# Mamba-2 scan with a cosine router: the start of the scan reordered, with work moved from VectorE and ScalarE to GpSimd

## The chip, the cores and the metric

The kernel runs on one core of one Trainium2 chip. The metric is the device time of one execution in microseconds (us), median of several runs. Before the change it is 239.88 us over three runs (239.1, 239.88 and 241.01).

The engines are TensorE (in the profile PE, and PEld for its weight loads), VectorE (DVE), ScalarE (ACT), GpSimd (POOL) and SyncE (SP), which here issues nearly all loads. Each engine works through its own queue in order. A wait in front of an instruction holds everything behind it on that engine.

## The reference, cut to what matters

Two blocks are chained: a state-space scan and a layer of eight experts.

```python
# scan; batch 4, heads 8, seq 768, head_dim 32, d_state 16
cum = np.cumsum(np.log(np.clip(a, 1e-06, 1.0)), axis=-1)      # within a chunk
M = np.einsum('bhin,bhjn->bhij', Cc, Bc) * np.exp(cum_i - cum_j) * causal
y = M @ xc + np.exp(cum_i) * (Cc @ state)
state = decay_full * state + sum_j(decay_from_j * Bc_j * xc_j)
# router and experts; 3072 tokens of 256, 8 experts with F = 1024
logits = normalize(x) @ normalize(expert_emb).T / tau
out[mask_e] = gate * (np.maximum(x[mask_e] @ w1[e], 0) @ w2[e])
```

The result does not depend on the length of the chunk, and the kernel uses chunks of 128 tokens (`Q`), so there are six of them (`NC`), for all four batches (`NB`) and eight heads at once.

## The kernel before, in words

**Two parts.** The scan, `mamba` (line 776), runs first and writes one row per token to DRAM. The experts, `moe`, follow: rows are gathered per expert and multiplied with its weights. The change touches the scan alone, and in it `begin_scan` (line 723), which prepares chunk 0, and the constants that are built there.

**How a chunk is computed.** The factor exp(cum_i - cum_j) is split in two. `decays` (line 242) turns the input `a` into products of decays `f`, taken from the middle of the chunk (`HQ` = 64), and `inverse` (line 267) takes 1/f as `r`, on VectorE. TensorE spreads `f` to the layout of C with a matrix of zeros and ones (`spread_decays`, line 283): four batches by four chunks are 16 matmuls, chunks 0 and 1 to the two banks of `py`, chunks 2 and 3 to the two of `pz`. `scale_c` (line 315) multiplies C by that on VectorE and gives `cp`. `turn_inverse` (line 273) transposes `r` on TensorE, and ScalarE copies it to `rT`. `scale_x` (line 324) multiplies x by it and gives `xs`.

Then come pairs of batches. Pair p is chunk p // 2, batches 0 and 1 or 2 and 3. For each pair:

- `scores` (line 607): 16 matmuls of B by `cp`, into the PSUM tiles `pgA` and `pgB`. B stands in `bz` in two copies, each with the rows of the other half zeroed. For chunks 0 and 1 `split_b` (line 226) makes the copies on ScalarE from a plain load `in_b`, by a multiplication with the masks `tmask`. From chunk 2 on, DMAs of single rows write straight into `bz`, which `clear_b` (line 156) zeroed on ScalarE.
- `masks` (line 620): the causal mask. VectorE multiplies `pgA` by the mask. ScalarE copies `pgB` to the SBUF tile `g`, and GpSimd zeroes the upper triangle there (`affine_select`, line 631).
- `outputs` (line 636): 16 matmuls (32 records, each fp32 matmul is two passes) of `xs` by `g` into `py`. From the third record pair on they need GpSimd's half of `g`.
- `sums` (line 670), once per chunk: B by `xs`, which gives the new state, and `tokens` (line 701), which turns the outputs to rows.

The next pair's `scores` write `pgA` and `pgB` again, so they wait until `masks` of this pair has read them.

**What sets the order.** The order on each engine is the order in which the code calls these functions (a hand-made schedule); waits are put in by the framework. `begin_scan` (lines 744 to 773) issues, in this order: the constants of the later routing (`place_consts`, all on GpSimd), the decays, `split_b(0)`, the spread, `inverse`, `scale_c(0)` for two batches and two more, `scale_x(0)`, `scores(0)`, some fill matmuls on zeros (line 239), the squares of the router's embeddings (line 363, ScalarE, and a power on GpSimd, line 364), `masks(0)`, `split_b(1)`, `scale_c(1)`, `scores(1)`, `masks(1)`.

**Loads.** SP issues them in the order of the calls, and a load may also wait for the load eight places earlier, because eight semaphores are used in turn. `in_b`, `in_c` and `in_x` are B, C and x of a chunk in the layouts of the scan; `in_t` is B by token.

## Time and profile before

| | |
|---|---|
| median of three runs | 239.88 us (239.1 to 241.01) |
| the profiled execution | 238.6 us, of which the span of the trace is 236.9 us |
| granted TensorE clock, mean | 0.992 of full speed |
| busy, share of the span | PE 95%, DVE 75%, ACT 54%, POOL 41% |
| instructions | 6602 |

The rows of the trace are read so: start in us from the span's start, duration in us, engine, line of the code, operation, output <- input with partitions x elements, and the number of merged instructions. In square brackets stands how long the engine had been idle and what ended that. "Mean ns" in a grouped row is the mean duration of one instruction. A row for a DMA shows the issue; its landing is in a view of its own.

### The profile page before, as it was taken

Reading aid. Unit: us, or ns where it says so; the run is one execution under the profiler, and the core shown is the slowest. Engines: PE = TensorE matmul, PEld = TensorE weight load, DVE = VectorE, ACT = ScalarE, POOL = GpSimd, SP = SyncE. Lnnn points to the kernel's source line nnn. Section 1 sums busy time; section 2 is a strip of 40 time slices with the busy share of each in tenths; the row PEclk is TensorE's granted clock in tenths of the full one; section 3 lists DMA queues with packets and bytes.
Section 4 is the critical chain, followed back from the end, with each engine's and each line's share of the span. In section 5 each row is a group of like instructions: output and inputs, shape, how many; then the busy total and the mean of one; then the engine's idle time right before and its main releaser. Section 6 shows DMA issues by size and latency. Waiting matters only on the chain. (4 is left out here: it accounts for less than half of the span.)

```text
span 236.9 us, 6602 instructions
## 1 busy us (share of the span) xinstructions
PE 224.1 (95%) x2500; PEld 211.2 (89%) x2500; DVE 178.5 (75%) x468; ACT 129.0 (54%) x348; POOL 98.0 (41%) x125
## 2 busy tenths in 40 slices
PE   7899989999999799999999999999999999999980
PEld 7788878877899699999999999999999999999970
DVE  6997968997875628697868788877887978874850
ACT  6867665762621445653684468358456456647620
POOL 8736211263027507536427334631841643305113
PEclk9999999999999999999999999999999999999996
DMA  5879675565607832626246233724626444201002
GB/s 176 280 230 299 236 185 163 155 196 164 233 13 261 295 116 69 209 75 187 78 148 190 82 133 114 238 63 166 192 80 203 144 140 148 93 3 61 0 3 64
DMA packets 20978, 34.83 MB, mean 147 GB/s; under 512 B 2474, under 2 KB 13968, under 8 KB 20944
## 3 DMA queue, kind: packets, MB, share of 16 engines
q1 hardware_dynamic: 18256, 27.97, 36.9%
q0 software_dynamic: 2592, 6.39, 8.5%
q8 instruction: 20, 0.33, 0.6%
q14 instruction: 14, 0.11, 0.2%
q10 hardware_dynamic: 96, 0.03, 0.1%
HBM read 28.02 MB, written 6.42 MB: 145 GB/s over the span
## 5 line engine op out<-in xcount | busy, mean ns | idle before, releaser
L1135 POOL DMA_INDIRECT out_dram<-yo,to x26 | 29.4, 1130 | 60.7 <-ACT yo L1134 46.4
L1058 DVE TENSOR_TENSOR hT<-bank,hp 128x416 f32<-128x416 f32 (+6 forms) x42 | 22.1, 553 | 14.8 <-ACT hp L1052 9.7
L908 POOL DMA_INDIRECT xg<-rows,table x24 | 27.9, 1162 | 7.0 <-issue 4.5
L1052 ACT COPY hp<-bank 128x416 f32<-128x416 f32 (+6 forms) x42 | 19.9, 475 | 17.7 <-PE bank L1039 17.3
L1064 ACT ACTIVATE hT<-hT 128x416 f32<-128x416 f32 (+6 forms) x42 | 21.6, 525 | 11.3 <-DVE hT L1058 11.2
L1000 DVE TENSOR_TENSOR ws<-w 128x512 f32<-128x512 f32 x42 | 27.6, 685 | 0.0
L631 POOL TENSOR_SCALAR_AFFINE_SELECT g<-g 128x1024 f32<-128x1024 f32 x13 | 16.3, 1257 | 25.9 <-ACT g L630 25.9
L1039 PE MATMUL bank<-ts,w 128*128 128x208 f32 (+6 forms) x112 | 21.8, 328 | 0.0
L1039 PE MATMUL bank<-xT,w 128*128 128x208 f32 (+6 forms) x112 | 21.6, 326 | 0.0
L1100 PE MATMUL bank<-ts,w 128*128 128x208 f32 (+6 forms) x112 | 21.4, 334 | 0.0
L1039 PE MATMUL bank<-ts,ws 128*128 128x208 f32 (+6 forms) x112 | 20.5, 326 | 0.0
L1100 PE MATMUL bank<-ts,ws 128*128 128x208 f32 (+6 forms) x112 | 19.5, 326 | 0.0
L1100 PE MATMUL bank<-hT,w 128*128 128x208 f32 (+6 forms) x112 | 19.5, 326 | 0.0
L1100 PEld LDWEIGHTS bank<-ts,w 128*128 128x128 f32 x112 | 18.1, 190 | 0.9 <-DVE ts L1004 0.2
L1004 DVE TENSOR_TENSOR ts<-hT 128x416 f32<-128x416 f32 (+6 forms) x28 | 15.0, 556 | 5.1 <-ACT hT L1064 4.1
L1039 PEld LDWEIGHTS bank<-xT,w 128*128 128x128 f32 x112 | 18.8, 190 | 0.0
L1039 PEld LDWEIGHTS bank<-ts,ws 128*128 128x128 f32 x112 | 18.5, 190 | 0.1
L923 POOL TENSOR_TENSOR gr<-gr,half 128x3 f32<-128x3 f32 (+2 forms) x9 | 9.2, 1022 | 22.4 <-ACT sq L919 13.2
L1039 PEld LDWEIGHTS bank<-ts,w 128*128 128x128 f32 x112 | 18.0, 190 | 0.5 <-ACT hp L1052 0.4
L1100 PEld LDWEIGHTS bank<-hT,w 128*128 128x128 f32 x112 | 18.4, 190 | 0.0
L1100 PEld LDWEIGHTS bank<-ts,ws 128*128 128x128 f32 x112 | 18.4, 190 | 0.0
L1004 DVE TENSOR_TENSOR ts<-hT,ts 128x416 f32<-128x416 f32 (+6 forms) x28 | 14.9, 551 | 0.2
(256 smaller groups left out, 496.5 us busy)
## 6 DMA issues: line engine op xcount, KB each, us to landing
w<-in_moe_w_dram SPq DMA_DIRECT2D x28, 512.0 KB, 3.5
rows<-yt SPq DMA_DIRECT2D x12, 264.0 KB, 2.9
in_x<-in_x_dram SPq DMA_DIRECT2D x6, 512.0 KB, 5.0
w<-in_moe_w_dram SPq DMA_DIRECT2D x8, 256.0 KB, 3.6
in_c<-in_CT_dram SPq DMA_DIRECT2D x6, 256.0 KB, 4.2
in_t<-in_B_dram SPq DMA_DIRECT2D x6, 256.0 KB, 3.7
bz<-in_BT_dram SPq DMA_DIRECT2D x16, 64.0 KB, 4.9
in_b<-in_BT_dram SPq DMA_DIRECT2D x2, 256.0 KB, 3.3
```

Source lines behind the costliest of these rows:

```text
L631: nc.gpsimd.affine_select(out=g, in_=g, pattern=[[0, 8], [1, Q]], compare_op=ALU.is_ge, fill=0.0, base=0, channel_multiplier=-1)
L908: s.k.nc.gpsimd.indirect_dma_start(out=s.x[0:p, i, 0:TOK], out_offset=None, in_=rows, in_offset=bass.IndirectOffsetOnAxis(ap=s.at[0:p, i : ...
L923: nc.gpsimd.tensor_tensor(out=s.r[:], in0=s.r[:], in1=k.half[:, 0:nt], op=ALU.pow)
L1000: s.k.nc.vector.tensor_tensor(out=o, in0=in0, in1=in1, op=op)
L1004: s.k.nc.vector.tensor_tensor(out=t[i], in0=in0, in1=in1, op=ALU.subtract)
L1039: k.nc.tensor.matmul(out[:, g], lhsT=lhsT[:, f : f + 128], rhs=rhs, start=(g == 0 and i in (1, 2, 5)), stop=True, skip_group_check=True,)
L1052: nc.scalar.copy(out=u.p[:, {1: 0, 6: 1, 7: 2}[i]], in_=u.a)
L1058: nc.vector.tensor_tensor(out=out, in0=in0, in1=u.p[:, q], op=ALU.add)
L1064: s.k.nc.scalar.activation(c, c, ACT.Relu)
L1100: k.nc.tensor.matmul(out, lhsT=lhsT, rhs=rhs, start=(i in (1, 2) and f == 0), stop=(f == half - 1), skip_group_check=True)
L1135: d = nc.gpsimd.indirect_dma_start(out=k.out[:, :], out_offset=bass.IndirectOffsetOnAxis(ap=s.to[0:p, i : i + 1], axis=0), in_=y[:p], in_o ...
```

## The change

**First decays.** `spread_decays` takes the batches to be spread. Batches 0 and 1 are spread first, for chunks 0 to 3, then 2 and 3. Of chunk 0, batches 0 and 1 go to `pgA[:, 0]`, a bank that nothing else uses then. VectorE scales C for batches 0 and 1 from there, and for 2 and 3 from `py`. Four matmuls of one column (`spread_last`) bring the last decay of chunk 0 to `py`, where the copy to `fr` reads it.

**Inverse in two pieces.** The reciprocal is taken for columns 0 to 63 before the first `scale_c` and for 64 to 127 after the second one. The transposition comes after `scores(0)`, in a place of `pz[0]`.

**Order of VectorE.** `masks(0)` and `scale_c(1)` stand ahead of `scale_x(0)`. VectorE does the half of `xs` for batches 0 and 1, GpSimd the half for 2 and 3. The copy of one column of C for chunk 1 goes from VectorE to ScalarE.

**GpSimd.** It makes the two copies of B of chunk 1 (`split_b` with `scalar=False`), ahead of its first mask. The constants of the routing are no longer built at the start but in four portions after the masks of steps 2 to 5.

**Zeroing of `bz`.** Before: two copies on ScalarE of 1024 elements per partition. Now one of 1536 on ScalarE, at the start, and a memset of 512 on VectorE.

**Loads.** x of chunk 0 comes in two halves, and B of chunk 1 is loaded before C of chunk 1.

The core of the diff:

```diff
-    clear_b(k, 2)
+    k.nc.scalar.copy(
+        out=k.bz[:, 2:4].rearrange("p c v b m -> p (c v b) m")[:, 0 : 3 * NB], in_=bc(k.zero[:, 0:Q], [128, 3 * NB, Q], 1)
+    )
...
+    v.memset(k.bz[:, 3, 1].rearrange("p b m -> p (b m)"), 0.0)
...
+        h = m // 2 if n == "x" and c == 0 else m
+        for o in range(0, m, h):
+            k.nc.sync.dma_start(v[:].rearrange("p b m -> p (b m)")[:, o : o + h], src[:, o : o + h])
...
-def split_b(k, c):
+def split_b(k, c, scalar=True):
...
+        if scalar:
+            k.nc.scalar.activation(t.bz[:, v], t.bt[:], ACT.Copy, scale=k.tmask[:, v : v + 1])
+        else:
+            flat = lambda a: a.rearrange("p b m -> p (b m)")
+            k.nc.gpsimd.tensor_scalar(
+                out=flat(t.bz[:, v]), in0=flat(t.bt[:]), scalar1=k.tmask[:, v : v + 1], scalar2=None, op0=ALU.mult
+            )
...
-def inverse(k, kk):
+def inverse(k, kk, cut=slice(0, Q)):
...
+def spread_last(k):
     for b in range(NB):
+        k.nc.tensor.matmul(
+            k.py[:, 0, b : b + 1], lhsT=k.spread[0:32, b, :], rhs=k.f[0:32, 0, Q - 1 : Q], start=True, stop=True,
+            tile_position=(0, 0),
+        )
...
+            at = k.pgA[:, 0] if c == 0 and b < 2 else spread_at(k, c)
...
-def scale_x(k, c, lo=0, n=NB):
+def scale_x(k, c, lo=0, n=NB, vector=True):
...
-    load(k, 1, "cb")
+    load(k, 1, "bc")
...
-    turn_consts(k)
-    next(consts)
-    next(consts)
     next(first)
     next(first)
+    inverse(k, 0, slice(0, HQ))
     split_b(k, 0)
-    clear_b(k, 3)
     load_two(k, 2)
-    spread_decays(k, range(4))
-    inverse(k, 0)
-    scale_c(k, 0, spread_at(k, 0), 0, 2)
-    turn_inverse(k, 0, k.pgB[:, 1, 384:512])
+    turn_consts(k)
+    split_b(k, 1, scalar=False)
+    spread_decays(k, range(4), (0, 1))
+    scale_c(k, 0, k.pgA[:, 0], 0, 2)
+    spread_decays(k, range(4), (2, 3))
     scale_c(k, 0, spread_at(k, 0), 2, 2)
-    scale_x(k, 0)
-    scores(k, 0)
+    inverse(k, 0, slice(HQ, Q))
     keep_decays(k, 2)
     keep_decays(k, 3)
+    scores(k, 0)
+    spread_last(k)
+    masks(k, 0)
+    turn_inverse(k, 0, k.pz[0][:, 384:512])
     fill(k, 3, k.pz[0][:, 0:Q])
...
-    norm_embeddings(k)
-    masks(k, 0)
-    split_b(k, 1)
     scale_c(k, 1, spread_at(k, 1))
     t = k.ld[1]
-    nc.vector.tensor_copy(out=t.cp[:, :, HQ : HQ + 1], in_=t.ct[:, :, HQ : HQ + 1])
+    nc.scalar.copy(out=t.cp[:, :, HQ : HQ + 1], in_=t.ct[:, :, HQ : HQ + 1])
+    scale_x(k, 0, 0, 2)
+    scale_x(k, 0, 2, 2, vector=False)
+    norm_embeddings(k)
     scores(k, 1)
     masks(k, 1)
-    k.later = later
+    k.later, k.consts = later, consts
...
         if 1 < s and not last:
             masks(k, s, () if s in (3, 9) else (1,))
+        if 1 < s:
+            next(k.consts, None)
```

How the instructions stand on three queues. The names left of the arrow are outputs; the waits are the semaphores that stand in front of an instruction. On VectorE, from the last step of the decays (`f`) to the mask of pair 1, before:

```order
L263 MEMSET f 32x1 [waits DVE_49]
L269 RECIPROCAL r<-f 128x128 [waits DVE_49]
L270 MEMSET r 128x1 [waits DVE_49]
L321 TENSOR_TENSOR cp<-in_c,py 128x256 [waits DMAHW5_49,PE_49]
L321 TENSOR_TENSOR cp<-in_c,py 128x256
L330 TENSOR_TENSOR xs<-in_x,rT 128x1024 [waits DMAHW6_49,Activation_49]
L628 TENSOR_TENSOR g<-pgA,mask 128x1024 [waits PE_49,Pool_49]
L321 TENSOR_TENSOR cp<-in_c,py 128x512 [waits DMAHW3_49,Activation_49]
L770 COPY cp<-in_c 128x4 [waits DVE_49]
L628 TENSOR_TENSOR g<-pgA,mask 128x1024 [waits PE_49]
```

and now:

```order
L277 MEMSET f 32x1 [waits DVE_49]
L283 RECIPROCAL r<-f 128x64
L346 TENSOR_TENSOR cp<-in_c,pgA 128x256 [waits DMAHW5_49,PE_49]
L346 TENSOR_TENSOR cp<-in_c,py 128x256 [waits PE_49]
L283 RECIPROCAL r<-f 128x64 [waits DVE_49]
L285 MEMSET r 128x1 [waits DVE_49]
L653 TENSOR_TENSOR g<-pgA,mask 128x1024 [waits PE_49,Pool_49]
L346 TENSOR_TENSOR cp<-in_c,py 128x512 [waits DMAHW5_49,PE_49,Activation_49]
L355 TENSOR_TENSOR xs<-in_x,rT 128x512 [waits DMAHW6_49]
L653 TENSOR_TENSOR g<-pgA,mask 128x1024 [waits PE_49]
```

`xs` has moved from ahead of the first mask to behind the scaled C of chunk 1, and only half of it is left; the copy of one column is gone.

On GpSimd, around its first mask of the scan (`g`), before:

```order
L125 IOTA step_i 128x32
L127 CAST step<-step_i 128x32 [waits Pool_49]
L151 MEMSET width 128x1 x8
L364 TENSOR_TENSOR emb_r<-emb_r,half 8x1 [waits Activation_49]
L631 AFFINE_SELECT g<-g 128x1024 [waits Activation_49] x2
```

and now:

```order
L381 COPY turn<-ident 128x2x32 x2
L242 TENSOR_SCALAR bz<-in_b_154,tmask 128x512 [waits DMAHW4_49]
L242 TENSOR_SCALAR bz<-in_b_154,tmask 128x512
L656 AFFINE_SELECT g<-g 128x1024 [waits Activation_49]
L355 TENSOR_TENSOR xs<-in_x,rT 128x512 [waits DMAHW7_49,Activation_49]
L389 TENSOR_TENSOR emb_r<-emb_r,half 8x1 [waits Activation_49,Pool_49]
L656 AFFINE_SELECT g<-g 128x1024 [waits Activation_49]
```

The constants are gone from the stretch; the two copies of B, with a wait for a load, stand ahead of the first mask, and half of `xs` ahead of the second.

On SP, the loads behind those of x of chunk 0, before:

```order
L347 DMA tau<-in_moe_tau_dram 8x1 [waits DMAHW2_49]
L177 DMA in_c<-in_CT_dram 128x512 [waits DMAHW3_49]
L177 DMA in_b_160<-in_BT_dram 128x512 [waits DMAHW4_49]
L177 DMA in_t<-in_B_dram 128x512 [waits DMAHW5_49]
L166 DMA a_92<-in_a_dram 32x128 [waits DMAHW6_49]
```

and now:

```order
L372 DMA tau<-in_moe_tau_dram 8x1 [waits DMAHW3_49]
L185 DMA in_b_154<-in_BT_dram 128x512 [waits DMAHW4_49]
L185 DMA in_c<-in_CT_dram 128x512 [waits DMAHW5_49]
L185 DMA in_t<-in_B_dram 128x512 [waits DMAHW6_49]
L172 DMA a_92<-in_a_dram 32x128 [waits DMAHW7_49]
```

The load of C of chunk 1 now waits for semaphore 5, which the load of C of chunk 0 raises; before, B by token (`in_t`) stood at that wait.

More of the change, by code (lines that the diff above doesn't have):

```diff
@@ L106, in early_consts, with late_consts @@
     )
-    before = m.tile([128, 128], F32, name="before")
+    k.half = c.tile([128, NU], F32, name="half")
+    g.memset(k.half[:], 0.5)
+def late_consts(k):
+    c, g = k.const, k.nc.gpsimd
+    before = k.mc.tile([128, 128], F32, name="before")
     g.affine_select(
-        out=before[:], in_=ones[:, 0:128], pattern=[[1, 128]], compare_op=ALU.is_gt, fill=0.0, base=0,
+        out=before[:], in_=k.ones[:, 0:128], pattern=[[1, 128]], compare_op=ALU.is_gt, fill=0.0, base=0,
         channel_multiplier=-1,
     )
-    k.half = c.tile([128, NU], F32, name="half")
-    g.memset(k.half[:], 0.5)
     k.ones_b = c.tile([128, 128], BF16, name="ones_b")
@@ L128, in ramp @@
         return f
+    k.xg = [c.tile([128, NT, 2 * Y1], F32, name=f"xg{i}") for i in range(3)]
+    late_consts(k)
+    yield
     k.lows = ramp("lows", 128, BF16)
@@ L142, in place_consts @@
     nc.gpsimd.memset(k.acc[:], 0.0)
+    yield
     k.shift_f = c.tile([128, E], F32, name="shift_f")
@@ L151, in place_consts @@
         nc.gpsimd.memset(k.width[:, r : r + 1], float(w + PAD if r == 0 else w))
-    k.xg = [c.tile([128, NT, 2 * Y1], F32, name=f"xg{i}") for i in range(3)]
     yield
-def clear_b(k, i):
-    k.nc.scalar.copy(out=k.bz[:, i], in_=bc(bc(k.zero[:, 0:Q], [128, NB, Q], 1), [128, 2, NB, Q], 1))
 def load_decays(k, c, engine):
@@ L229, in split_b @@
     for v in range(2):
-        k.nc.scalar.activation(t.bz[:, v], t.bt[:], ACT.Copy, scale=k.tmask[:, v : v + 1])
+        if scalar:
[5 more added lines that the diff above has]
+            )
 def fill(k, n, at=None):
@@ L264, in decays @@
     yield
-def inverse(k, kk):
+def inverse(k, kk, cut=slice(0, Q)):
     p = slice(0, 64 if kk else 128)
-    k.nc.vector.reciprocal(out=k.r[p, kk], in_=k.f[p, kk])
-    k.nc.vector.memset(k.r[p, kk, HQ : HQ + 1], 1.0)
+    k.nc.vector.reciprocal(out=k.r[p, kk, cut], in_=k.f[p, kk, cut])
+    if cut.stop == Q:
+        k.nc.vector.memset(k.r[p, kk, HQ : HQ + 1], 1.0)
 def turn_inverse(k, kk, ps):
@@ L280, in spread_at, with spread_decays @@
     return (k.py[:, 0], k.py[:, 1], k.pz[0], k.pz[1], k.py[:, 0], k.py[:, 1])[c]
-def spread_decays(k, chunks):
+def spread_last(k):
     for b in range(NB):
+        k.nc.tensor.matmul(
+            k.py[:, 0, b : b + 1], lhsT=k.spread[0:32, b, :], rhs=k.f[0:32, 0, Q - 1 : Q], start=True, stop=True,
+            tile_position=(0, 0),
+        )
+def spread_decays(k, chunks, batches=range(NB)):
+    for b in batches:
         for c in chunks:
             g = 32 * (c % 4)
+            at = k.pgA[:, 0] if c == 0 and b < 2 else spread_at(k, c)
             k.nc.tensor.matmul(
-                spread_at(k, c)[:, 128 * b : 128 * b + 128], lhsT=k.spread[g : g + 32, b, :],
+                at[:, 128 * b : 128 * b + 128], lhsT=k.spread[g : g + 32, b, :],
                 rhs=k.f[g : g + 32, c // 4, :], start=True, stop=True, tile_position=(g, 0),
@@ L329, in scale_x @@
     r = k.rT[:, c // 4, 32 * (c % 4) + 8 * lo : 32 * (c % 4) + 8 * lo + 8 * n]
-    k.nc.vector.tensor_tensor(
+    (k.nc.vector if vector else k.nc.gpsimd).tensor_tensor(
         out=t.xs[:, b].rearrange("p b h d -> p (b h) d"), in0=t.x[:, b].rearrange("p b (h d) -> p (b h) d", h=NH),
@@ L744, in begin_scan @@
     first, later, consts = decays(k, 0), decays(k, 1), place_consts(k)
-    turn_consts(k)
-    next(consts)
-    next(consts)
     next(first)
     next(first)
+    inverse(k, 0, slice(0, HQ))
     split_b(k, 0)
-    clear_b(k, 3)
     load_two(k, 2)
-    spread_decays(k, range(4))
-    inverse(k, 0)
-    scale_c(k, 0, spread_at(k, 0), 0, 2)
-    turn_inverse(k, 0, k.pgB[:, 1, 384:512])
+    turn_consts(k)
[3 more added lines that the diff above has]
+    spread_decays(k, range(4), (2, 3))
     scale_c(k, 0, spread_at(k, 0), 2, 2)
-    scale_x(k, 0)
-    scores(k, 0)
+    inverse(k, 0, slice(HQ, Q))
     keep_decays(k, 2)
     keep_decays(k, 3)
+    scores(k, 0)
+    spread_last(k)
+    masks(k, 0)
+    turn_inverse(k, 0, k.pz[0][:, 384:512])
     fill(k, 3, k.pz[0][:, 0:Q])
-    nc.scalar.copy(out=k.fr[:, 0, :, Q - 1 : Q], in_=by_batch(spread_at(k, 0))[:, :, Q - 1 : Q])
+    nc.scalar.copy(out=k.fr[:, 0, :, Q - 1], in_=k.py[:, 0, 0:NB])
     nc.scalar.copy(out=k.fr[:, 1, :, HQ:Q:63], in_=by_batch(spread_at(k, 1))[:, :, HQ:Q:63])
-    norm_embeddings(k)
-    masks(k, 0)
-    split_b(k, 1)
     scale_c(k, 1, spread_at(k, 1))
     t = k.ld[1]
-    nc.vector.tensor_copy(out=t.cp[:, :, HQ : HQ + 1], in_=t.ct[:, :, HQ : HQ + 1])
+    nc.scalar.copy(out=t.cp[:, :, HQ : HQ + 1], in_=t.ct[:, :, HQ : HQ + 1])
+    scale_x(k, 0, 0, 2)
+    scale_x(k, 0, 2, 2, vector=False)
+    norm_embeddings(k)
     scores(k, 1)
     masks(k, 1)
-    k.later = later
+    k.later, k.consts = later, consts
 def mamba(k):
```

1 line of the change is left out of this document (removed).

## The prediction

> **What bounds the kernel now.** I read the busy time by stretches of the span first (us of the stretch, then busy time and instructions of PE, PEld, DVE, ACT and POOL, granted clock, DMA share, GB/s).
>
> ```profile
> 16.00:68.00 52.00, 49.98 (x1248) 42.91 (x1248) 42.96 (x102) 30.09 (x58) 15.29 (x12) 1.00 0.61 189
> 68.00:231.00 163.00, 160.65 (x996) 156.50 (x995) 122.61 (x332) 87.05 (x269) 69.43 (x61) 1.00 0.40 127
> ```
>
> From 16 us on TensorE is busy 96% and then 99% of the time at full clock. So whatever moves the start of that stretch moves the end by as much, and nothing else in this change can. The price of the change is how much earlier or later TensorE gets into its unbroken run. That is read from the timeline of the first 16 us:
>
> ```profile
> 6.42 0.75 DVE L321 TENSOR_TENSOR cp<-in_c,py 128x256 f32<-128x256 f32 x2
> 6.99 0.38 PE L614 MATMUL pgA<-cp,bz 32*128 32x128 f32 x2 [0.27 <-DVE cp L321]
> 7.37 1.23 DVE L330 TENSOR_TENSOR xs<-in_x,rT 128x1024 f32<-128x1024 f32 x1 [0.20 <-DMA in_x<-in_x_dram]
> 7.96 0.28 PE L614 MATMUL pgB<-cp,bz 32*128 32x128 f32 x2
> 8.17 0.94 PE L239 MATMUL pz<-zero 128*128 128x128 f32 x6
> 8.40 0.98 ACT L630 COPY g<-pgB 128x1024 f32<-128x1024 f32 x1
> 8.52 1.22 DVE L628 TENSOR_TENSOR g<-pgA,mask 128x1024 f32<-128x1024 f32 x1
> 9.25 0.58 POOL L364 TENSOR_TENSOR emb_r<-emb_r,half 8x1 f32<-8x1 f32 x1
> 9.65 0.68 DVE L321 TENSOR_TENSOR cp<-in_c,py 128x512 f32<-128x512 f32 x1
> 9.79 0.38 PE L614 MATMUL pgA<-cp,bz 32*128 32x128 f32 x2 [0.69 <-DVE g L628]
> 9.81 1.09 POOL L631 TENSOR_SCALAR_AFFINE_SELECT g<-g 128x1024 f32<-128x1024 f32 x1
> 10.36 0.56 DVE L770 COPY cp<-in_c 128x4 f32<-128x4 f32 x1
> 10.89 1.13 PE L657 MATMUL py<-g,xs 128*32 128x128 f32 x32
> 11.00 1.23 DVE L628 TENSOR_TENSOR g<-pgA,mask 128x1024 f32<-128x1024 f32 x1
> ```
>
> The chain is: scaled C at 6.42, scores(0) from 6.99 to 8.24 (7.96 + 0.28), VectorE's mask from 8.52, because `xs` holds VectorE until 8.60, to 9.74, scores(1) at 9.79. TensorE's last real wait is the 0.69 us ahead of 9.79; the fill matmuls at 8.17 are also waiting. From 9.79 it runs on: outputs(0) at 10.89, which needs GpSimd's part of the mask, done at 9.81 + 1.09 = 10.90. The same timeline a little later:
>
> ```profile
> 12.14 1.09 POOL L631 TENSOR_SCALAR_AFFINE_SELECT g<-g 128x1024 f32<-128x1024 f32 x1 [1.24 <-ACT g L630]
> 12.39 0.38 PE L614 MATMUL pgA<-cp,bz 32*128 32x128 f32 x2
> 13.50 0.65 PE L657 MATMUL py<-g,xs 128*32 128x128 f32 x16
> 14.05 1.22 DVE L628 TENSOR_TENSOR g<-pgA,mask 128x1024 f32<-128x1024 f32 x1
> 14.79 1.09 POOL L631 TENSOR_SCALAR_AFFINE_SELECT g<-g 128x1024 f32<-128x1024 f32 x1 [1.57 <-ACT g L630]
> 15.18 0.98 DVE L695 TENSOR_TENSOR T<-V,whole 128x256 f32<-128x256 f32 x1
> ```
>
> Scores(2) start at 12.39 and outputs(1) at 13.50, with GpSimd's second mask done at 13.23, in time. I carry the sum to these places.
>
> **The change part by part.** First the loads, since two instructions now wait for them (issue rows, then the median from issue to landing of single loads: C of chunk 0, x of chunk 0, B of chunk 1):
>
> ```profile
> 2.16 0.43 SPq L177 DMA_DIRECT2D in_c<-in_CT_dram  x1
> 2.64 0.43 SPq L177 DMA_DIRECT2D in_x<-in_x_dram  x1
> 4.96 0.43 SPq L177 DMA_DIRECT2D in_b<-in_BT_dram  x1
> in_c<-in_CT_dram SPq DMA_DIRECT2D x1, 256.0 KB, 3.9
> in_x<-in_x_dram SPq DMA_DIRECT2D x1, 512.0 KB, 4.6
> in_b<-in_BT_dram SPq DMA_DIRECT2D x1, 256.0 KB, 4.1
> ```
>
> C of chunk 0 lands at 2.16 + 3.9 = 6.06, x at 7.24, B of chunk 1, queued behind C of chunk 1, at 9.06.
>
> *First decays by batch.* Scaled C for batches 0 and 1 no longer waits for all 16 spread matmuls, but cannot start before C is there: 6.10 instead of 6.42. The gain is 0.32, not the half of the spread. Scores(0) followed 0.57 after it (6.42 to 6.99) and took 1.25, so they run 6.67 to 7.92. Splitting the inverse takes the second half off this path; it lies under scores(0).
>
> *Mask ahead of `xs`.* The mask starts when scores(0) end, at about 8.05 (gain 0.47), and ends at 9.27; scores(1) start at 9.32. The four matmuls of one column and the moved transposition stand in TensorE's wait, ahead of the fill; between 7.92 and 9.32 there are 1.40 us, of which the fill takes 0.94. If they take more than the remaining 0.46, scores(1) slip: 0 at best, 0.2 at worst. I take 0, because the step below comes out later in any case.
>
> *GpSimd.* Its queue is now: two copies of B (128x512), mask, half of `xs`, power, mask. B of chunk 1 has moved one place forward. C and B of chunk 1 are equal in size and landed between 7.24 and 9.06, so I put the first at half way, 8.15, and the bounds at 7.6 and 9.06; C now takes the second place, 9.06, just before it is needed at 9.27. For the copies there is no row. The nearest ones, and the two that show ScalarE's side and VectorE's prices:
>
> ```profile
> 2.99 0.29 POOL L97 TENSOR_SCALAR_AFFINE_SELECT ident<-ident 128x128 f32<-128x128 f32 x1
> 9.29 1.33 ACT L230 ACTIVATE bz<-in_b,tmask 128x512 f32<-128x512 f32 x2
> 17.69 0.69 DVE L321 TENSOR_TENSOR cp<-in_c,fr 128x512 f32<-128x512 f32 x1
> 23.90 0.41 DVE L695 TENSOR_TENSOR T<-V,whole 128x256 f32<-128x256 f32 x1
> 26.90 1.09 POOL L631 TENSOR_SCALAR_AFFINE_SELECT g<-g 128x1024 f32<-128x1024 f32 x1 [3.09 <-ACT g L630]
> 27.03 2.04 DVE L330 TENSOR_TENSOR xs<-in_x,rT 128x1024 f32<-128x1024 f32 x1
> ```
>
> From 0.29 at 128 elements to 1.09 at 1024 a copy of 512 takes 0.65; half of 1.09, 0.54, and 0.75 are the bounds. Two copies: 8.20 to 9.50. ScalarE's part of the mask, which is no longer behind the transposed inverse, ends at 8.05 + 0.98 = 9.03. So GpSimd's mask runs 9.50 to 10.59, against 10.90 before. What was taken from ScalarE (1.33) has become GpSimd's bound.
>
> *VectorE against GpSimd.* The rows show that the two engines exclude each other on some operations. `T` takes 0.41 alone (23.90), but 0.98 when it meets a mask on GpSimd: 14.79 + 1.09 = 15.88, and `T` ends at 16.16, 0.28 later. `xs` takes 1.23 alone and 2.04 at 27.03: it ends 1.08 after GpSimd's mask does. The little copy at 10.36 took 0.56 and ended with GpSimd's mask. The mask on VectorE, which reads PSUM, keeps its 1.22 at 14.05. So an operation of VectorE with both inputs in SBUF stands still until GpSimd's instruction is over, and saves some 0.13 of its start. The Trainium skill, "SBUF — State Buffer", section "Who interferes with whom", states it as a rule: a VectorE instruction with two SBUF inputs and a GpSimd instruction that reads SBUF share a read port, and the one that issues second blocks fully. By that rule the new half of `xs` cannot lie under GpSimd's mask; without it the half would cost its 0.69 and no more. The rows above bear the rule out.
>
> VectorE has scaled C of chunk 1 by 9.18 + 0.69 = 9.87 and would start its half of `xs` at 9.9. GpSimd's mask began at 9.50, so it waits until 10.59 and ends at 10.59 + 0.69 - 0.13 = 11.15. Outputs(0) need it: they start at 11.25 instead of 10.89, a loss of 0.36. The gain of 0.47 is not lost ahead of that point but is spent in this wait. Mask(1) then runs 11.15 to 12.38, ahead of scores(2) at 12.39 + 0.36 = 12.75.
>
> *Half of `xs` on GpSimd.* It comes after VectorE's half. It reads two tensors of 512, as many elements as the mask's 1024, so I take 1.09; bounds 0.65 (one input) and 1.3 (two such). 11.15 to 12.24, before the second half of the sums needs it at about 12.5. The power, 0.58, ends at 12.82 and the second mask at 13.91. Outputs(1) start at 13.50 + 0.36 = 13.86 and need it with their third matmul: another 0.1. With the bounds of the half this is 0 to 0.3. The Trainium skill, "GPSIMD Engine Reference", section 3.1, gives 4497 ns for a two-input operation of 2048 elements, about twice VectorE; a quarter of that is 1.12 by estimate, and the sum would stay. No row of this trace has such an operation on GpSimd.
>
> *Hidden edits.* The constants of the routing were GpSimd's work from 3.77 to 9.30, with no one waiting. Their first and last rows, two gaps ahead of later masks, and two rows for the zeroing of `bz`:
>
> ```profile
> 3.11 1.03 ACT L157 COPY bz<-zero 128x1024 f32<-128x1024 f32 x1
> 3.34 0.23 DVE L250 TENSOR_SCALAR aw<-a 128x126 f32<-128x126 f32 x1 [0.87 <-DMA a<-in_a_dram]
> 3.77 0.40 POOL L108 TENSOR_SCALAR_AFFINE_SELECT before<-ones 128x128 f32<-128x128 f32 x1
> 8.96 0.34 POOL L151 MEMSET width<- 128x1 f32 x8
> 18.50 3.00 POOL L631 TENSOR_SCALAR_AFFINE_SELECT g<-g 128x1024 f32<-128x1024 f32 x2 [2.62 <-ACT g L630]
> 22.73 1.09 POOL L631 TENSOR_SCALAR_AFFINE_SELECT g<-g 128x1024 f32<-128x1024 f32 x1 [1.22 <-ACT g L630]
> ```
>
> At most 5.5 us in four portions, some 1.4 each at the longest, go into gaps of which these two and the 3.09 above are three. If a portion of 1.4 met the gap of 1.22, that mask would be 0.2 late; I take 0. ScalarE's zeroing of 1536 elements takes about half as long again, 3.11 to 4.66, and its two copies of B of chunk 0, 1.33, end at 6.0, ahead of scores(0); if they were later than 6.67, each 0.1 would cost as much. VectorE's memset lies in the 0.87 us of waiting for `a`. The extra load costs SP one issue of 0.43; B of chunk 1 is issued where C stood, plus that, and both wait behind x of chunk 0 anyway.
>
> **The sum.** -0.47 up to the first mask, +0.83 for the wait of `xs` (from -0.47 to +0.36), +0.1 at the second mask of GpSimd: +0.46. The profiled execution took 238.6 us (span 236.9) and would take 239.06. The median of the three runs shown, 239.88, is 1.28 above that execution, so I forecast 239.88 + 0.46, rounded to 240.3 us.
>
> **The rivals.**
>
> *A, the forecast:* GpSimd's queue takes the place of ScalarE's and VectorE's. 240.3 us.
>
> *B, the gain comes through.* If B of chunk 1 lands at the early bound, 7.6, and each copy takes 0.54, GpSimd's mask starts at 9.08 with ScalarE's and ends at 10.17. The half of `xs` ends at 10.73, outputs(0) start at 10.83, near 0. If the half also gets in ahead of that mask, it ends at 10.6 and the gain is up to 0.47, less what the second mask gives back. For it speaks that scores(0) really start earlier; against it the 9.06 of the load. Between 0 and -0.47 I put it at -0.3: 239.6 us.
>
> *C, the port goes the wrong way.* If GpSimd's next instruction, its own half of `xs`, is served at 10.59 ahead of the waiting half of VectorE, this one begins 1.09 later, ends at 12.24, and outputs(0) start at 12.34: +1.45, so 241.3 us. It decides as soon as VectorE's half arrives while the mask of GpSimd is running, as in A. The rows show VectorE waiting behind a single instruction of GpSimd, never behind two in a row, so they cannot exclude it.
>
> *D, the change does nothing:* the moved matmuls and the fill push scores(1) back to 9.8 and what remains cancels. 239.9 us. For it speaks the narrow 0.46; against it that the fill has only to end, not to be followed by a wait.
>
> **How the numbers follow.** A 0.45, B 0.30, C 0.15, D 0.10. All four lie within 0.7% of 239.88. A measurement of this kernel can tell about 1% from no change (2.4 us), and its three runs lie 1.9 us apart. The range takes in B and C and half of that scatter: 238.9 to 241.6. Beyond 1% only something outside these cases would reach: 0.04 for faster, 0.05 for slower (C together with copies at 0.75 and a late load), 0.91 within.
>
> **What would show it.** In the profile of the changed kernel: scaled C at about 6.1, scores(0) at 6.7, scores(1) at 9.3. If A holds, VectorE's half of `xs` is a row of 1.2 us that ends half a us after GpSimd's mask, outputs(0) start at 11.2, and the idle time of GpSimd between its first two masks is gone. If that row is 0.6 to 0.7 and outputs(0) start before 10.9, B is right. If GpSimd's `xs` ends ahead of VectorE's, C is. A stretch from 16 us on that is shorter or longer by more than 0.3 us would show that I was wrong to look at the start alone.

## The result and the profile after

| | before | after |
|---|---|---|
| median, same chip | 239.85 us (6 runs, 239.1 to 241.01) | 243.14 us (6 runs, 241.64 to 243.85) |
| ratio, with 95% interval | | 1.0122 (1.0091 to 1.0154) |
| profiled execution, span | 238.6 us, 236.9 us | 242.41 us, 240.7 us |
| busy share of the span: PE, DVE, ACT, POOL | 95%, 75%, 54%, 41% | 94%, 74%, 53%, 44% |

The change costs 1.2%, about 2.9 us. The forecast was 240.3 us with a range up to 241.6, so the time lies outside it, on the slow side.

To see where the time went I followed one event through both traces, the start of the scores of each pair on TensorE. The start of the kernel comes first. These are rows of the timeline of the changed kernel (start and duration in us, engine, line, operation, output <- input; in brackets the idle time before and what ended it):

```profile
6.62 0.42 DVE L346 TENSOR_TENSOR cp<-in_c,pgA 128x256 f32<-128x256 f32 x1 [1.09 <-PE pgA L312]
7.19 0.38 PE L639 MATMUL pgA<-cp,bz 32*128 32x128 f32 x2
8.46 1.23 DVE L653 TENSOR_TENSOR g<-pgA,mask 128x1024 f32<-128x1024 f32 x1 [0.17 <-PE pgB L639]
8.75 3.15 POOL L242 TENSOR_SCALAR bz<-in_b,tmask 128x512 f32<-128x512 f32 x2 [4.08 <-DMA in_b<-in_BT_dram]
9.40 0.27 ACT L291 COPY rT<-pz 128x128 f32<-128x128 f32 x1
9.72 0.94 PE L253 MATMUL pz<-zero 128*128 128x128 f32 x6 [0.35 <-ACT rT L291]
10.45 1.11 DVE L355 TENSOR_TENSOR xs<-in_x,rT 128x512 f32<-128x512 f32 x1
10.58 0.38 PE L639 MATMUL pgA<-cp,bz 32*128 32x128 f32 x2
11.70 0.41 PE L682 MATMUL py<-g,xs 128*32 128x128 f32 x4
11.85 1.10 POOL L656 TENSOR_SCALAR_AFFINE_SELECT g<-g 128x1024 f32<-128x1024 f32 x1
12.92 1.05 POOL L355 TENSOR_TENSOR xs<-in_x,rT 128x512 f32<-128x512 f32 x1
13.00 0.96 PE L682 MATMUL py<-g,xs 128*32 128x128 f32 x26 [0.89 <-POOL g L656]
14.45 0.38 PE L639 MATMUL pgA<-cp,bz 32*128 32x128 f32 x2
```

The rows of GpSimd (POOL) and the last rows of TensorE (PE) tell it. GpSimd spends 3.15 us on two copies of B that were forecast at 1.30. Its first mask therefore starts at 11.85 instead of the forecast 9.50. Outputs(0) begin at 11.70, run out of masked scores after four records and stand still until 13.00. Scores(2) start at 14.45; before, they started at 12.39. So 2.06 us are lost by there.

The forecast held that nothing after the first 16 us could change. The busy time by stretches of the changed kernel (same columns as before: PE, PEld, DVE, ACT, POOL) and the list of what TensorE waited for between 5 and 60 us say otherwise:

```profile
16.00:68.00 52.00, 48.94 (x1249) 41.37 (x1240) 43.12 (x94) 30.54 (x58) 23.45 (x42) 1.00 0.61 190
```
```profile
PE py L682 <- POOL g L656: 0.9, 1, 0.9
PE pgA L639 <- DVE g L653: 0.8, 1, 0.8
PE py L682 <- issue: 0.4, 1, 0.4
```

GpSimd works 23.45 us there instead of 15.29, TensorE 48.94 instead of 49.98. The first wait is the one above. The second stands at the scores of pair 5:

```profile
20.55 3.19 POOL L656 TENSOR_SCALAR_AFFINE_SELECT g<-g 128x1024 f32<-128x1024 f32 x2 [0.96 <-ACT g L655]
23.52 0.30 DVE L264 TENSOR_SCALAR aw<-a 64x126 f32<-64x126 f32 x1
24.58 0.21 POOL L134 CAST his<-his_i 128x32 f32<-128x32 int32 x1
24.79 1.09 POOL L656 TENSOR_SCALAR_AFFINE_SELECT g<-g 128x1024 f32<-128x1024 f32 x1
24.84 1.04 DVE L275 TENSOR_TENSOR f<-w,at 64x1 f32<-64x1 f32 x1
25.81 1.21 DVE L653 TENSOR_TENSOR g<-pgA,mask 128x1024 f32<-128x1024 f32 x1
27.07 0.38 PE L639 MATMUL pgA<-cp,bz 32*128 32x128 f32 x2 [0.79 <-DVE g L653]
```

VectorE meets GpSimd's mask at 24.79 with an operation on one column, `f<-w,at`. With both inputs in SBUF it takes 1.04 us, until that mask is over. VectorE's own mask follows behind it, and TensorE waits 0.79 us. The same place before the change:

```profile
21.46 0.21 DVE L250 TENSOR_SCALAR aw<-a 64x126 f32<-64x126 f32 x1
22.70 0.14 DVE L261 TENSOR_TENSOR f<-w,at 64x1 f32<-64x1 f32 x1
22.73 1.09 POOL L631 TENSOR_SCALAR_AFFINE_SELECT g<-g 128x1024 f32<-128x1024 f32 x1 [1.22 <-ACT g L630]
```

The mask itself is not late: 24.79 is 22.73 plus the 2.06 us that were lost already, although a portion of constants (its last row is the one at 24.58) ends just ahead of it. VectorE is late, by less than a tenth of a us. The two masks ahead take 3.19 us, from 20.55, instead of 3.00, from 18.50, and `aw<-a`, which meets their end, takes 0.30 instead of 0.21. So `f<-w,at` starts 0.05 behind the mask and not 0.03 ahead of it, and stands still for the whole mask. In all four kernels with late constants the two masks take 3.19 or 3.20 us and one operation on `f` 1.04 to 1.12. In the other ten profiles, all with the constants at the start, the two masks take 2.86 to 3.02, and no operation on `f` stands still.

The starts of scores(p) in all profiles that the argument uses, as shifts in us against the first profile of before (6.99, 9.79, 12.39, 20.32, 24.16, 39.46, 43.95 and 52.55); the first column of numbers is the point, in us of the span and to some 0.2 us, at which TensorE's full clock began (4.3 in that first profile). It is read from the matmuls: those that spread the decays take 0.42 us each ahead of that point and 0.28 behind it. The granted clock in the profile's own stretches reads 1.00 on both sides and does not show it.

| kernel | clock from | (0) | (1) | (2) | (4) | (5) | (8) | (9) | (11) |
|---|---|---|---|---|---|---|---|---|---|
| after | 6.8 | +0.20 | +0.79 | +2.06 | +2.06 | +2.91 | +2.91 | +3.46 | +3.46 |
| copies of B on ScalarE | 7.2 | +0.20 | +0.79 | +0.77 | +0.76 | +1.61 | +1.61 | +2.16 | +2.16 |
| constants first | 5.5 | -0.24 | +0.35 | +2.79 | +2.79 | +2.79 | +2.82 | +2.83 | +2.83 |
| both | 6.8 | +0.19 | +0.79 | +0.76 | +0.75 | +1.94 | +3.69 | +3.70 | +3.70 |
| copies by another operation | 5.7 | -0.17 | +0.42 | +1.62 | +1.62 | +2.48 | +2.49 | +2.82 | +2.81 |
| both, fill in its own bank | 4.5 | -0.41 | +0.18 | +0.79 | +0.79 | +2.33 | +2.54 | +2.55 | +2.55 |
| both, no fill | 5.9 | -0.04 | -0.29 | +1.17 | +1.17 | +1.27 | +2.94 | +2.94 | +2.94 |
| both, no fill, C first | 6.7 | +0.20 | -0.06 | +0.39 | +0.38 | +0.38 | +0.44 | +0.45 | +0.46 |
| the same, x in one load | 5.4 | -0.29 | -0.55 | -0.11 | -0.11 | +0.59 | +2.28 | +2.29 | +2.28 |
| before, copies moved | 5.8 | +0.39 | +0.14 | +0.25, then held | +1.73 | +2.47 | +2.47 | +2.48 | +2.48 |
| before, constants moved | 7.4 | +1.07 | +0.82 | +0.79 | +0.96 | +1.91 | +1.92 | +1.92 | +1.93 |
| before, prices of GpSimd at the end | 4.5 | +0.10 | +0.00 | +0.01 | +0.01 | +0.01 | +0.01 | +0.01 | +0.01 |
| before, second profile | 7.3 | +1.06 | +0.81 | +0.79 | +0.78 | +1.26 | +3.07 | +3.08 | +3.08 |

The last row, the control, is the one to read first: the same code can start up to 1.06 us later and lose 3 us by the end of the scan. What an edit did is a difference of rows at equal clock, or a wait that has a name in the trace.

### The profile page after: what moved, and what is told of

Read it like the earlier page. It is cut to its first block, busy times and chain, and to the rows that moved or that the text cites. A ratio compares the mean times of both kernels' runs of the same rounds, so it can differ in the third digit from the quotient of the medians.

```text
span 240.7 us, 6620 instructions
## 1 busy us (share of the span) xinstructions
PE 226.8 (94%) x2508; PEld 213.3 (89%) x2508; DVE 178.9 (74%) x469; ACT 127.7 (53%) x346; POOL 104.7 (44%) x128
## 5 line engine op out<-in xcount | busy, mean ns | idle before, releaser
L656 POOL TENSOR_SCALAR_AFFINE_SELECT g<-g 128x1024 f32<-128x1024 f32 x13 | 17.2, 1332 | 18.1 <-ACT g L655 18.1
L682 PE MATMUL py<-g,xs 128*32 128x128 f32 x384 | 14.0, 276 | 1.3 <-POOL g L656 0.9
```

The lines of the kernel that those rows point to most:

```text
L656: nc.gpsimd.affine_select(out=g, in_=g, pattern=[[0, 8], [1, Q]], compare_op=ALU.is_ge, fill=0.0, base=0, channel_multiplier=-1)
L682: nc.tensor.matmul(k.py[g : g + 32, v, 128 * i : 128 * i + 128], lhsT=t.xs[:, b + i, 4 * v + q, :], rhs=s.g[:, q, 2 * i + v, :], start=(c ...
```

## The experiments

Ratios are against the kernel before on the same chip. Its median was between 239.37 and 242.18 us there, so ratios, not times, are compared.

**The copies of B back on ScalarE.**

```diff
-    split_b(k, 1, scalar=False)
...
+    split_b(k, 1)
     scale_c(k, 1, spread_at(k, 1))
```

> The changed kernel, but the two copies of B of chunk 1 are made by ScalarE again, behind its two copies to fr. Theory (the copies of B on GpSimd, 3.15 us instead of the 1.3 forecast, hold its first mask until 12.95): GpSimd's mask ends near 10.6, the 0.89 us wait of TensorE in outputs(0) is gone, scores(2) start at 13.0 to 13.3 instead of 14.45, and the median falls by 1.2 to 2 us, to 241 to 242. Rival (TensorE's slow clock in the first 7 us and the late fill matmuls, which put scores(1) at 10.58, carry the loss): scores(2) stay at 14 or later, median 242.5 to 243.

243.17 us, ratio 1.0026 (0.9996 to 1.0057). GpSimd's first mask and scores(2) in its timeline:

```profile
9.52 1.10 POOL L656 TENSOR_SCALAR_AFFINE_SELECT g<-g 128x1024 f32<-128x1024 f32 x1 [4.96 <-DMA a<-in_a_dram]
11.68 1.08 PE L682 MATMUL py<-g,xs 128*32 128x128 f32 x32
13.16 0.38 PE L639 MATMUL pgA<-cp,bz 32*128 32x128 f32 x2
```

The mask starts at 9.52 instead of 11.85, outputs(0) run through in one piece, and scores(2) come at 13.16 instead of 14.45. The copies on GpSimd cost 1.29 us at this place, and the rival, by which scores(2) stay at 14 or later, is out. In time more came off than that, 0.96% or 2.3 us; each of the two ratios is known to about 0.3%, so 1.3 is not excluded. The jumps at scores(5) and (9) stay.

**The constants first.** The four portions at the start, as before the change; everything else as changed.

```diff
     turn_consts(k)
+    for _ in consts:
+        pass
```

> The changed kernel, but GpSimd builds all constants of the routing at the start again, where it otherwise waits 4.1 us for B of chunk 1. Theory (the portions of constants between the masks block VectorE and make its masks late): the waits of scores(5) on VectorE's mask (0.8 us) and of outputs(7) on GpSimd go, the shift against the kernel before stays what it is at scores(2) from there to the experts, and the median falls by 1.0 to 1.5 us, to 241.6 to 242.1. Rival (these waits come from the late start, which changes how the masks of the two engines meet): the waits stay, median 243 or a little above.

244.0 us, ratio 1.0072 (1.0041 to 1.0103). The copies and what waits for them, from its timeline:

```profile
9.14 3.50 POOL L242 TENSOR_SCALAR bz<-in_b,tmask 128x512 f32<-128x512 f32 x2 [0.41 <-DMA in_b<-in_BT_dram]
12.59 1.09 POOL L656 TENSOR_SCALAR_AFFINE_SELECT g<-g 128x1024 f32<-128x1024 f32 x1
13.74 0.96 PE L682 MATMUL py<-g,xs 128*32 128x128 f32 x26 [1.99 <-POOL g L656]
```

The shift is +2.79 at scores(2) and stays within 0.04 us of that to the end, so both later jumps are gone. Scores(2) follow the end of the copies by 2.59 us here (12.59 to 15.18) and by 2.60 in the changed kernel (11.85 to 14.45): that end sets them, not what happens before it. The time falls by 0.5%, 1.2 us, as expected, though the intervals of the two ratios overlap a little.

**Both edits together.**

> Both edits: copies of B on ScalarE, constants at the start. If the two losses are separate they add: 2.4 to 3.3 us off, median 239.8 to 240.8, that is level with the kernel before within 0.4%. If what is left of the change (mask ahead of the scaled x, spread by batch, x in halves) gains, below 239.8; if the fill matmuls and the slow clock cost by themselves, 240.5 to 241.

242.67 us, ratio 1.0011 (0.998 to 1.0041). The time agrees: 1.1%, some 2.7 us, are off. With this run there are four kernels, with and without each of the two edits: 1.0122, 1.0026 (copies back), 1.0072 (constants first) and 1.0011 (both). Averaged over the two cases of the other edit, the copies cost 0.78%, 1.9 us, and the late constants 0.33%, 0.8 us; 0.3 us are left. By the intervals each of these estimates is good to about 0.7 us. So the copies are clear of no cost, the constants barely. The profile has neither named wait, but a wait of 0.99 us on TensorE at 23.2 us, with no releaser in the trace, and a window of 3.41 us at half clock; both are taken up with the control.

**The price of GpSimd's operations.** The kernel before, with instructions on GpSimd behind everything else, when no other engine works; the extra time is theirs and not compared.

```diff
+    for n in (128, 256, 512):
+        g.tensor_scalar(out=dst[:, 0:n], in0=src[:, 0:n], scalar1=k.part[:], scalar2=None, op0=ALU.mult)
+    g.tensor_scalar(out=dst, in0=src, scalar1=3.0, scalar2=None, op0=ALU.mult)
+    g.tensor_tensor(out=dst, in0=src, in1=two, op=ALU.mult)
+    g.tensor_tensor(out=dst, in0=src, in1=k.part[:].to_broadcast([128, 512]), op=ALU.mult)
+    g.tensor_copy(out=dst, in_=src)
...
```

> The kernel before, with eight extra instructions on GpSimd at its end, on data that nothing reads, to price them alone: tensor_scalar with a scalar per partition at 128, 256 and 512 elements, with an immediate at 512, tensor_tensor at 512 with a full and with a broadcast second input, a copy and an affine_select at 512. If the copies of B are dear by themselves, tensor_scalar at 512 takes 1.5 to 1.6 us and grows by about 3 ns per element; if they were slowed by VectorE in the changed kernel, 0.6 to 0.8 us. Copy and affine_select at 512: 0.6 to 0.7; tensor_tensor: 1.0 to 1.1. The total time is some 8 us longer than before or less and says nothing.

The three sizes of the first operation (shortest, median and longest, in ns), then 512 elements by other operations (the second number is us):

```profile
L1470 POOL TENSOR_SCALAR yt<-yt,part x3: 640/940/1562, 237.4 to 239.1; 128x128 f32<-128x128 f32 x1, 128x256 f32<-128x256 f32 x1, 128x512 f32<-128x512 f32 x1
```
```profile
242.35 1.26 POOL L1472 TENSOR_TENSOR yt<-yt 128x512 f32<-128x512 f32 x1
243.69 1.04 POOL L1473 TENSOR_TENSOR yt<-yt,part 128x512 f32<-128x512 f32 x1
244.80 0.61 POOL L1474 COPY yt<-yt 128x512 f32<-128x512 f32 x1
245.48 0.61 POOL L1475 TENSOR_SCALAR_AFFINE_SELECT yt<-yt 128x512 f32<-128x512 f32 x1
```

A copy of 512 elements times a scalar per partition takes 1.56 us with nothing beside it, and 1.58 in the changed kernel. So the copies are dear by themselves; VectorE does not slow them there. `affine_select`, the operation whose rows I took for the estimate, takes 0.61, and so does a plain copy.

**The copies by a cheaper operation.** `tensor_tensor` with the mask broadcast, 1.04 us each in the row above, instead of 1.56.

```diff
-            k.nc.gpsimd.tensor_scalar(
-                out=flat(t.bz[:, v]), in0=flat(t.bt[:]), scalar1=k.tmask[:, v : v + 1], scalar2=None, op0=ALU.mult
+            k.nc.gpsimd.tensor_tensor(
+                out=flat(t.bz[:, v]), in0=flat(t.bt[:]), in1=k.tmask[:, v : v + 1].to_broadcast([128, NB * Q]), op=ALU.mult
```

> The changed kernel, with its two copies of B on GpSimd as tensor_tensor with the mask broadcast instead of tensor_scalar: priced alone 1.04 against 1.56 us. Theory (the price of these two instructions holds the first mask): GpSimd's first mask starts 1.0 us earlier, the wait of TensorE in outputs(0) nearly goes, and 0.9 to 1.1 us come off the time (0.4%), ratio to the kernel before 1.008 if the changed kernel is 1.012. Rival (the copies are slow because VectorE holds the port, whatever the instruction): no change.

241.54 us, ratio 1.0081 (1.0053 to 1.0109). The ratio is the expected one, though its interval overlaps that of the changed kernel. The rival is out: the copies take 2.04 us together instead of 3.15. But the wait in outputs(0) does not nearly go: 0.45 us for GpSimd's mask are left, and 0.31 for VectorE's half of `xs` come to it. Two copies that are 0.52 us shorter each should bring scores(2) 1.04 us earlier; they come 0.44 us earlier. The rows show why:

```profile
8.97 2.04 POOL L242 TENSOR_TENSOR bz<-in_b,tmask 128x512 f32<-128x512 f32 x2 [4.39 <-DMA in_b<-in_BT_dram]
10.21 1.35 DVE L355 TENSOR_TENSOR xs<-in_x,rT 128x512 f32<-128x512 f32 x1
10.96 1.55 POOL L656 TENSOR_SCALAR_AFFINE_SELECT g<-g 128x1024 f32<-128x1024 f32 x1
```

The load is 0.22 us later, and the mask takes 1.55 us instead of 1.10, because VectorE's half of `xs`, held until the copies were over (10.21 to 11.56), now holds the mask.

**The copies alone.** The kernel before; only the two copies of B of chunk 1 on GpSimd, in the place of `split_b(1)`, behind the first mask.

```diff
-        k.nc.scalar.activation(t.bz[:, v], t.bt[:], ACT.Copy, scale=k.tmask[:, v : v + 1])
+        if c == 0:
+            k.nc.scalar.activation(t.bz[:, v], t.bt[:], ACT.Copy, scale=k.tmask[:, v : v + 1])
+        else:
...
```

> The kernel before, with nothing changed but the two copies of B of chunk 1, made by GpSimd with the same instruction, behind its first mask. At 1.56 us each they run from 10.9 to 14.0: scores(2), which need them, start at 14.1 instead of 12.4, and GpSimd's second mask ends at 15.1 instead of 13.2. Expected +1.7 to +2.0 us, ratio 1.007 to 1.009. If ScalarE's freed 1.3 us gave something back, less; if the price were the 0.65 of the forecast, +0.1.

241.19 us, ratio 1.0075 (1.0041 to 1.011), as expected. Here TensorE waits for the copies themselves, inside the scores of pair 2, which begin at 12.64 and are held after their first part:

```profile
14.21 0.38 PE L620 MATMUL pgA<-cp,bz 32*128 32x128 f32 x2 [1.06 <-POOL bz L234]
```

The copies run from 11.01 to 14.15, and GpSimd's second mask ends at 15.25 (15.1 expected).

**The constants alone.** The kernel before; only the four portions behind the masks of steps 2 to 5.

> The kernel before with one edit: GpSimd's constants in four portions behind the masks of steps 2 to 5, as in the change. Theory: a portion and a mask do not fit into one gap, so a mask or an operation of VectorE comes late and TensorE waits, whatever the start looks like: +0.85 and +0.55 in the kernel after, so 0.5 to 1.4 us here, ratio 1.002 to 1.006, with jumps of the shift between scores(4) and scores(9) and none before. Rival: in the kernel after the portions cost only because its start was already late; then the ratio is 1.000 +- 0.002 and no jump is seen.

243.12 us, ratio 1.0038 (1.001 to 1.0067). Its timeline at the same place as in the changed kernel:

```profile
23.68 1.09 POOL L641 TENSOR_SCALAR_AFFINE_SELECT g<-g 128x1024 f32<-128x1024 f32 x1 [0.22 <-ACT g L640]
23.71 1.12 DVE L270 TENSOR_SCALAR f<-f,w 64x64 f32<-64x64 f32 x1
24.81 1.21 DVE L638 TENSOR_TENSOR g<-pgA,mask 128x1024 f32<-128x1024 f32 x1
26.07 0.38 PE L624 MATMUL pgA<-cp,bz 32*128 32x128 f32 x2 [0.41 <-DVE g L638]
```

The same mechanism without the rest of the change: an operation of VectorE (64 elements, 0.25 us in the changed kernel) stands still under GpSimd's mask, and scores(5) wait 0.41 us. GpSimd was idle for 0.22 us ahead of that mask, so the portion did fit into the gap; what came late is VectorE. From scores(2) to (5) the shift grows by 1.12 us, in the control by 0.47, with an equal unnamed wait of 0.28 in both; by this comparison the constants cost 0.65 us there. The theory holds for the jump at (5). It fails for the one at (9), which does not appear here. In time this run cannot be told from the control (1.0025).

**The fill in a bank of its own.** With both edits above, the three fill matmuls behind the transposed inverse write `pz[1]` instead of `pz[0]`, which ScalarE reads.

```diff
-    fill(k, 3, k.pz[0][:, 0:Q])
+    fill(k, 3, k.pz[1][:, 0:Q])
```

> Copies of B on ScalarE and constants at the start, and the three fill matmuls go to the other bank of pz, so that they need not wait until ScalarE has copied the transposed inverse out of theirs. Theory (what is left of the loss, scores(1) at 10.1 to 10.6 instead of 9.3, is the fill that starts late and then stands ahead of scores(1)): scores(1) start within 0.15 us of the end of VectorE's mask, 0.5 to 0.9 us come off against the kernel with the copies and constants put back, ratio to the kernel before 0.998 or below. Rival (the slow clock of TensorE at the start, which depends on when its window ends, explains scores(1)): no change, 1.001.

240.62 us, ratio 1.0033 (1.0007 to 1.0059). The fill still waits 0.35 us for ScalarE's copy of the inverse, and scores(1) start 0.91 us after VectorE's mask (9.06 to 9.97), so this edit did not free them. The profile shows what comes next instead:

```profile
9.79 0.69 DVE L346 TENSOR_TENSOR cp<-in_c,py 128x512 f32<-128x512 f32 x1 [0.72 <-DMA in_c<-in_CT_dram]
9.98 1.05 POOL L355 TENSOR_TENSOR xs<-in_x,rT 128x512 f32<-128x512 f32 x1
10.39 1.19 DVE L355 TENSOR_TENSOR xs<-in_x,rT 128x512 f32<-128x512 f32 x1
11.73 1.08 PE L682 MATMUL py<-g,xs 128*32 128x128 f32 x32 [0.58 <-DVE xs L355]
```

VectorE waits 0.72 us for C of chunk 1, which is now loaded behind B. By then GpSimd has begun its half of `xs`, and VectorE's half ends 0.55 us after that one (11.58 against 11.03). This is the mechanism of rival C, in this kernel and not in the changed one.

**No fill.** With both edits, and the fill left out (it computes nothing that is used).

> As the one with the fill in its own bank, but without these three fill matmuls. If the fill only costs by standing ahead of scores(1), the same time as with its own bank. If it serves to keep TensorE's clock up, rows at half speed appear in some profiles and the time is 0.5 us or more above that.

241.16 us, ratio 1.003 (0.9992 to 1.0068). The time is that of the run before, so a price of leaving the fill out does not show. Its profile has a window at half clock, but so have those of "both" and of the control, which keep the fill. Scores(1) start at 9.50, 0.29 earlier than in before, but C comes later still:

```profile
10.45 0.69 DVE L346 TENSOR_TENSOR cp<-in_c,py 128x512 f32<-128x512 f32 x1 [1.00 <-DMA in_c<-in_CT_dram]
12.10 1.08 PE L682 MATMUL py<-g,xs 128*32 128x128 f32 x32 [1.43 <-DVE xs L355]
```

**C of chunk 1 first.** As the last one, with the loads in the order of before.

```diff
-    load(k, 1, "bc")
+    load(k, 1, "cb")
```

> The change with the copies of B back on ScalarE, the constants at the start, no fill, and C of chunk 1 loaded ahead of B again. Theory: with the fill gone scores(1) start at 9.5, and what held scores(2) at 13.56 without the fill was C of chunk 1, landed at 10.4 because it waited for C of chunk 0; with C first it lands at about 9, VectorE scales it at 9.2 to 9.4, the half of xs follows, and scores(2) start at 12.0 to 12.6: ratio 0.998 to 1.001. Rival: the port between VectorE's and GpSimd's halves of xs holds scores(2), whatever C does: then they start at 13 or later and the ratio stays at 1.003.

243.09 us, ratio 1.0043 (1.0012 to 1.0075). In the profile VectorE no longer waits for C, and scores(2) start at 12.78, 0.78 us earlier than without this edit and just later than the 12.0 to 12.6 expected. The time does not follow: the ratio is above the expected 0.998 to 1.001. The profiled execution, 241.63 us, was the fastest of its twelve, so this profile shows the kernel at its best.

**The same, with x of chunk 0 in one load.**

> As the run with C first, and x of chunk 0 in one load instead of two, which gives each later load the semaphore that it had before the change. Theory: C of chunk 1 is no longer late in the run with C first, so this changes nothing: within 0.2 us at scores(2), ratio 0.998 to 1.001. Rival: C is still late there because one more load stands ahead of it on SP; then scores(2) come 0.4 us earlier or more here.

243.3 us, ratio 1.0042 (1.0011 to 1.0073). Scores(2) come 0.50 us earlier, but so do scores(0), 0.49 us, as the clock began earlier: C was not late, and the load is not what moved them. This profile is the best view of the reordered start with an early clock:

```profile
6.13 0.42 DVE L346 TENSOR_TENSOR cp<-in_c,pgA 128x256 f32<-128x256 f32 x1 [0.49 <-PE pgA L312]
6.70 0.38 PE L639 MATMUL pgA<-cp,bz 32*128 32x128 f32 x2
9.24 0.38 PE L639 MATMUL pgA<-cp,bz 32*128 32x128 f32 x2 [0.38 <-DVE g L653]
9.95 0.73 DVE L355 TENSOR_TENSOR xs<-in_x,rT 128x512 f32<-128x512 f32 x1
10.10 1.48 POOL L355 TENSOR_TENSOR xs<-in_x,rT 128x512 f32<-128x512 f32 x1
```

Scores(1) start 0.55 us earlier than in before. Of that, 0.11 is left at scores(2), since outputs(0) wait until 10.82 (before 10.89).

**The control.** The kernel before, unchanged.

> The kernel before, unchanged, as a control. The full TensorE clock began 4.3 us into the span in the profile of before and between 4.5 and 7.4 us in the others. Theory: that is drawn anew in every execution, and the spread matmuls take 0.42 us instead of 0.28 as long as it has not begun; so a second profile of the same code starts scores(0) anywhere from 6.9 to 8.1, and shifts of up to 1 us against the first profile that are there at scores(0) already are not the work of an edit. The ratio should be 1.000 +- 0.003. Rival: the later clock is the changed code's doing; then this profile repeats 6.99, 9.79 and 12.39 to 0.1 us.

240.57 us, ratio 1.0025 (0.9996 to 1.0053). A spread matmul, scores(0) and scores(1) of this second profile:

```profile
7.02 0.42 PE L287 MATMUL py<-f,spread 32*128 32x128 f32 x2
8.05 0.38 PE L614 MATMUL pgA<-cp,bz 32*128 32x128 f32 x2 [0.34 <-ACT rT L276]
10.60 0.38 PE L614 MATMUL pgA<-cp,bz 32*128 32x128 f32 x2 [0.51 <-DVE g L628]
```

The rival is refuted: the same code starts scores(0) at 8.05 instead of 6.99, because its spread matmuls took 0.42 us to the end. Two things follow. The first profile of before had an early clock, and the changed kernel's +0.79 at scores(1) and what is left of it in "both" (+0.76 at scores(2)) is no more than what before itself does with a late one (+0.81, +0.79), though by another way: there scores(0) are late already, here the fill holds scores(1). And ratios up to about 1.005 cannot be told from no change here. The changed kernel lies clear of that; the copies alone (1.0075), the constants first (1.0072) and the other operation (1.0081) lie above it with intervals that just touch or overlap the control's; the rest cannot be told from it one by one.

## Why the prediction was wrong

**The kind was right, two sizes were not.** Forecast A said that GpSimd's queue takes the place of ScalarE's and VectorE's. It did: outputs(0) wait for GpSimd's mask. But the term that the sum put on this, "+0.83 for the wait of `xs`", did not occur in the changed kernel: VectorE's half of `xs` ended at 11.56, before GpSimd's mask began at 11.85, and what TensorE waited for was the mask. Where the copies are off GpSimd, the term came out: in the first experiment that mask ran from 9.52 to 10.62 (forecast 9.50 to 10.59) and VectorE's half ended at 11.16 (11.15). The start of that mask is a coincidence, as ScalarE's part set it there and not the copies. The time lay beyond all four cases. C was nearest with 241.3, but GpSimd's half of `xs`, which C lets go first, ran last, from 12.92.

**The copies, the step that failed first.** "From 0.29 at 128 elements to 1.09 at 1024 a copy of 512 takes 0.65; half of 1.09, 0.54, and 0.75 are the bounds." The rows were of `affine_select`, and for that operation the estimate was good (a straight line gives 0.63, and 0.61 was measured). The instruction is `tensor_scalar`, and it takes 1.58 us. Two of them are 1.85 us more than forecast, and the load landed at about 8.7 instead of 8.15, so they began 0.55 later: 2.40 us, of which the mask was late by 2.35 (11.85 against 9.50; its record starts 0.05 before the end of theirs). Scores(2) are 14.45 instead of 12.75. Taking the copies off GpSimd gave back 1.29 us there. The bounds were the real fault: they came from one operation, and the code names another. The trace of before had a hint in the row of `tmask` at 1.86: two `tensor_scalar` on GpSimd, of one element each, take 0.67 us together, more per instruction than the 0.29 of `affine_select` at 128.

**The constants, the second.** "If a portion of 1.4 met the gap of 1.22, that mask would be 0.2 late; I take 0." The mask was not late at all. VectorE was, by 0.08 us, and this moved its last operation on `f` from just ahead of the mask's start to just behind it, where it stood still for the mask's whole length. The step named the gap on GpSimd and not VectorE, which the moved work can hold up. It goes with a jump of 0.85 us at scores(5) in the changed kernel, of which 0.79 is the named wait, and with 0.65 alone; in time it is 0.8 us, give or take 0.7. With it falls the sentence that nothing behind the first 16 us can move the end; the prediction had named that stretch as its test.

**The start.** With an early clock and without the fill, the late constants, the copies on GpSimd and the new loads (the last but one experiment), the steps of the start came out close: scaled C 6.13 (forecast 6.10), scores(0) 6.70 (6.67), scores(1) 9.24 (9.32). GpSimd's half of `xs` took 1.05 alone and 1.48 to 1.49 where it met VectorE's (1.09 forecast, bounds 0.65 to 1.3). In the changed kernel itself the fill stood in the way, as rival D had it: it waits for ScalarE's copy of the transposed inverse and ends after VectorE's mask. At nearly the same clock scores(1) start at 10.58 with it and at 9.73 without, 0.85 us. With an early clock the fill holds them too: 9.97 in the run with the fill in its own bank. The term "I take 0" was wrong there too, but cost nothing, as the step behind it came later still.

**The sum.** Copies 1.29, scores(5) 0.85, scores(9) 0.55, and the start at 0 against before with an equally late clock: 2.7 us by the profiles, against 2.9 (2.2 to 3.7) measured. By the times of the four kernels it is 1.9 for the copies, 0.8 for the constants and 0.3 for the rest. The split agrees roughly; the share of scores(9) is counted, not explained.

**What stays open.** The 0.55 us at scores(9): a jump of 0.33 to 0.55 us appears there in all three kernels that have both the reordered start and the late constants, and in none with only one of them, though no constants are left by then; the wait on TensorE (0.40 in the changed kernel) has no releaser in the trace. The waits of 0.2 to 1.3 us with no releaser near 23 us, which the second profile of before has too (0.28): the DMA records have loads of instructions near there in every profile, with such a wait or without, and do not settle it. With them the shift at scores(5) also grows in kernels with the constants at the start, by 0 to 1.54 us; so the 0.85 of a single profile is not proof by itself, and the constants' part rests on the stopped operation of VectorE, which only the kernels with late constants show. And why the versions with a clean start are not faster: the profile of "C first" starts its last scores 2.6 us earlier than the second one of before (1.5 of them that one's window at half clock, and its execution was the fastest of twelve), but in time neither it nor any other version beat the kernel before.
